# A fused sliding-window attention and gMLP kernel: layout of the transposed x, clearing of the V ring, key evictions on two engines, and the place of the root steps

## The chip, the cores and the metric

The kernel runs on one core of one Trainium2 chip. The metric is the device time of one execution in microseconds, the median of three runs. The core has five engines with instruction streams of their own that wait for one another by semaphores: TensorE (PE in the profile, its weight loads PEld), VectorE (DVE), ScalarE (ACT), GpSimd (POOL) and SyncE (SP, which issues most DMA transfers here).

## The reference

```python
def _A_ref(x, wqkv, wo):                      # H = 32 heads of 16, W = 256
    qkv = (x @ wqkv).reshape(B, S, 3, H, Dh)  # S = 2048, D = 512
    scores = einsum('bhqd,bhkd->bhqk', q, k) * Dh ** -0.5
    scores = where(0 <= i - j < W, scores, -1e9)
    return einsum('bhqk,bhkd->bhqd', softmax(scores), v) @ wo
def _B_ref(x, w_in, w_sp, b_sp, w_out):       # F = 1376, Fh = 688
    z = gelu(x @ w_in)                        # tanh form
    z1, z2 = z[..., :Fh], layernorm(z[..., Fh:])
    g = einsum('ts,bsf->btf', w_sp, z2) + b_sp[None, :, None]
    return (z1 * g) @ w_out
xn = layernorm(x)
return x + _A_ref(xn, wqkv, wo) + _B_ref(xn, w_in, w_sp, b_sp, w_out)
```

All inputs are bfloat16.

## The kernel before

The 2048 tokens are 16 blocks of 128 (NB). The order of the instructions on each engine is written out by hand (`manual_schedule`): every engine executes its instructions in the order in which the Python code emits them, and the framework adds the semaphore waits that the tiles' reads and writes need. There are two parts.

**Prologue** (L230 to L438 of the source, inside one `with` that holds the PSUM pools ps_z and ps_t). x is loaded in pairs of blocks (L249 to L255) and w_in in four parts (c = 0 to 3, L258), two of them from ACT's queue and the rest from SP's. SP's queue then takes wqkv (L261), two transposed loads of w_sp (wspT, L221), wo (L264) and w_out (L265, L268). 14 matmuls on a zero tile `warm` run on PE meanwhile (L273).

For each block DVE takes mean and variance (`stat_steps`, L302 and L303), makes 1/sqrt and normalises x in place (L307). The first four blocks take the root from ACT (L347); blocks 4 to 15 take it four at a time from `rsqrt_steps` (L107), a chain of twelve small DVE instructions: three to set up (L111, L112, L116) and three Newton rounds (L123, L124, L128). `weave(a, b)` (L135) emits two lists alternately; the loop at L375 weaves the roots of one group with some statistics of the next. PE transposes the normalised block in four 128x128 pieces into a PSUM tile `tp` (L316) and ACT copies it to `xnT` (L319).

PE multiplies each block with w_in in two halves (`do_z`, `z_part`, L328: eight matmuls for one half of one block, called a z tile here), and ACT writes gelu of it to z1_all or z2_all (L344). The loop at L408 goes through the z tiles: both halves of blocks 1 to 8, then the second halves (z2) of 9 to 15, then their first halves. In it are dealt out:
- the transposes of later blocks;
- nine early units of the attention for the first 512 tokens: k0, q0, k1, q1, k2, q2, k3, q3 and v0 (`unit_k`, `unit_q`, `unit_v`; the number is the group of eight heads G). Each is four matmuls into a PSUM tile `me` from the same pool as `tp` (two banks, tag "t"), and evictions. A key unit is written twice to `k_ring`, for even and odd heads (e = 0, 1), each multiplied with a 0/1 column `emask`; in before both on DVE (L168). A query unit is copied by ACT (L183); v0 by DVE in four pieces (L202);
- the `side` list, one entry after each z tile from block 5: `clear_strips` (L95) zeroes strips of five E buffers, and `clear_v` (L224) zeroes one of five slots of the V ring and sets its columns of ones (L225, L227), all on DVE;
- the statistics of z2 (`z2_stats`, L207 and L208). After the eighth block the twelve root steps for blocks 0 to 7 follow in one piece (L429 in the print below), after the sixteenth those for 8 to 15, woven with the normalisation `z2_norm` (L211) of blocks 0 to 7.

The early evictions in before, as they stand:

```python
for e in range(2):
    dst = k_ring[:, G, o : o + 8, e, :]
    if on_act:
        nc.scalar.activation(out=dst, in_=m, func=ACT.Copy, scale=emask[:, e : e + 1])
    else:
        nc.vector.tensor_scalar(
            out=dst, in0=m, scalar1=emask[:, e : e + 1], scalar2=None, op0=ALU.mult
        )
...
u(a, 0, on_act=(u is unit_q), early=True)
```

**Main loop** (L650). 128 steps of two key half blocks each: four scores matmuls into S (`quad`, L534), exp by ACT into an E buffer (L544), a mask by DVE (L560), attention times V (`unit_av`, L575, L591, L592). A planner with fixed costs (C_P and so on, L604) fills PE between them with the remaining q, k and v units, the w_sp products (`unit_g`, L458, evicted at L464) and the output products (L492, L500, L504).

Of the kernel before, what the change touches and what calls it, by code (L numbers as in the profile page):

```python
# [8 lines left out]
P = 128  # L9
BF = mybir.dt.bfloat16  # L10
F32 = mybir.dt.float32
# [4 lines left out]
S_TOK = 2048  # L16
# [28 lines left out]
def kernel(  # L45
# [18 lines left out]
    ident = pers.tile([P, P], BF, name="ident")  # L64
    xnT = pers.tile([P, NDC, S_TOK], BF, name="xnT")
    wqkv = pers.tile([P, NDC, 3 * D], BF, name="wqkv")
# [7 lines left out]
    mask2 = pers.tile([P, 2, HK], BF, name="mask2")  # L74
    eps_t = pers.tile([P, 1], F32, name="eps_t")
    emask = pers.tile([P, 2], F32, name="emask")
    esel = pers.tile([P, 4], F32, name="esel")
# [75 lines left out]
    def unit_k(G, grp, on_act=False, early=False):  # L153
        m = m_tile(early=early)
        for c in range(NDC):
            nc.tensor.matmul(  # L156
                m, lhsT=wqkv[:, c, D + G * P : D + (G + 1) * P],
                rhs=xnT[:, c, grp * 512 : (grp + 1) * 512],
                start=(c == 0), stop=(c == NDC - 1),
            )  # L160
        o = (grp % 2) * 8
        m = m.rearrange("p (a k) -> p a k", k=HK)
        for e in range(2):
            dst = k_ring[:, G, o : o + 8, e, :]
            if on_act:
                nc.scalar.activation(out=dst, in_=m, func=ACT.Copy, scale=emask[:, e : e + 1])
            else:
                nc.vector.tensor_scalar(  # L168
                    out=dst, in0=m, scalar1=emask[:, e : e + 1], scalar2=None, op0=ALU.mult
                )  # L170

    def unit_q(G, grp, on_act=False, early=False):
        m = m_tile(early=early)
        for c in range(NDC):
            nc.tensor.matmul(  # L175
                m, lhsT=wqkv[:, c, G * P : (G + 1) * P],
                rhs=xnT[:, c, grp * 512 : (grp + 1) * 512],
                start=(c == 0), stop=(c == NDC - 1),
            )
        o = (grp % 2) * 512  # L180
        dst = q_ring[:, G, o : o + 512]
        if on_act:
            nc.scalar.copy(out=dst, in_=m)  # L183
        else:
            nc.vector.tensor_copy(out=dst, in_=m)

    def unit_v(n, on_act=False, early=False):
        m = m_tile(early=early)
        for c in range(NDC):
            nc.tensor.matmul(  # L190
                m, lhsT=xnT[:, c, n * P : (n + 1) * P], rhs=wqkv[:, c, 2 * D : 3 * D],
                start=(c == 0), stop=(c == NDC - 1),
            )
# [9 lines left out]

    def z2_stats(n):
        st = sml.tile([P, 2, nc.vector.BN_STATS_DIM], F32, name="st2")
        for j in range(2):
            nc.vector.bn_stats(out=st[:, j, :], in_=z2_all[:, n, j * 344 : (j + 1) * 344])  # L207
        nc.vector.bn_aggr(out=mv2[:, n, :], in_=st[:].rearrange("p a b -> p (a b)"))  # L208

# [13 lines left out]

    def clear_v(k):  # L224
        nc.vector.memset(v_ring[:, k], 0.0)  # L225
        for e in range(2):
            nc.vector.memset(v_ring[e * HK : (e + 1) * HK, k, :, :, e, DH : DH + 1], 1.0)  # L227


    with tc.tile_pool(name="win_pool", bufs=1) as winp, tc.tile_pool(  # L230
# [4 lines left out]
        w_in_sb = winp.tile([P, NDC, F], BF, name="w_in_sb")  # L235
        warm = winp.tile([P, 512], BF, name="warm")
        nc.vector.memset(warm[:], 0.0)
# [6 lines left out]
        for n2 in range(NB // 2):  # L244
# [11 lines left out]
            if n2 == 1:  # L256
                for c in range(NDC):
                    (nc.scalar if c < 2 else nc.sync).dma_start(  # L258
                        out=w_in_sb[:, c, :], in_=B_w_in[c * P : (c + 1) * P, :]
                    )  # L260
        nc.sync.dma_start(out=wqkv[:], in_=A_wqkv.rearrange("(c p) f -> p c f", p=P))  # L261
        load_wsp(0)
        load_wsp(1)
# [8 lines left out]
        for i in range(14):  # L272
            nc.tensor.matmul(wm[:], lhsT=warm[:, 0:P], rhs=warm[:], start=True, stop=True)  # L273

# [37 lines left out]
        def transpose_x(n):  # L312
            tp = ps_t.tile([P, NDC, P], BF, name="tp", tag="t")
            xn = xs_tiles.pop(n)
            for c in range(NDC):
                nc.tensor.transpose(  # L316
                    out=tp[:, c, :], in_=xn[:, c * P : (c + 1) * P], identity=ident[:]
                )
            nc.scalar.copy(out=xnT[:, :, n * P : (n + 1) * P], in_=tp[:])  # L319

# [4 lines left out]
        def z_part(zp, n, half, c):  # L325
            f0 = half * FH
            for lo, hi in Z_RANGES:
                nc.tensor.matmul(  # L328
                    zp[:, lo:hi],
                    lhsT=xnT[:, c, n * P : (n + 1) * P],  # L330
                    rhs=w_in_sb[:, c, f0 + lo : f0 + hi],
# [38 lines left out]
        norm_root(3)  # L370
        tiny = sml.tile([P, 1], F32, name="tiny")
        nc.scalar.activation(out=tiny[:], in_=eps_t[:], func=ACT.Gelu_apprx_tanh)

        weave(stat_steps(4, 8), [])
        for lo, hi, nxt in ((4, 8, 10), (8, 12, 14), (12, NB, NB)):  # L375
            weave(stat_steps(lo + 2 if lo > 4 else hi, hi), [])
            weave(rsqrt_steps(rstdx[:, lo:hi], mvx[:, lo:hi, 1], hi - lo), stat_steps(hi, nxt))
            for n in range(lo, hi):
                norm_apply(n)
            if lo == 4:  # L380
# [6 lines left out]
                )  # L387
                nc.vector.tensor_copy(out=b_all[:], in_=b_bf[:])

        early = [(unit_k, 0), (unit_q, 0), (unit_k, 1), (unit_q, 1), (unit_k, 2), (unit_q, 2),  # L390
                 (unit_k, 3), (unit_q, 3), (unit_v, 0)]
        side = [lambda eb=eb: clear_strips(eb) for eb in e_bufs]
        side += [lambda k=k: clear_v(k) for k in range(VRING)]
        stats_done = 0

        first = [(0, 0), (0, 1), (1, 0)]
        zt = [z_tile() for _ in first]
        for c in range(NDC):
            for zp, (n, half) in zip(zt, first):
                z_part(zp, n, half, c)  # L400
        transpose_x(2)
        for zp, (n, half) in zip(zt, first):
            gelu(n, half, zp)
        order = [(1, 1)] + [(n, h) for n in range(2, Z_BOTH) for h in range(2)]
# [3 lines left out]
        for i, (n, half) in enumerate(order):  # L408
# [5 lines left out]
            if n >= 6 and (half == 1 or i >= len(order) - 2) and early:  # L414
# [3 lines left out]
                else:  # L418
                    u(a, 0, on_act=(u is unit_q), early=True)
            if n >= 5:  # L420
                if side:
                    side.pop(0)()
                ready = n if half == 1 else (n if n < Z_BOTH else NB)
                for _ in range(1 if half == 0 and n < Z_BOTH else 2):
                    if stats_done < ready:
                        z2_stats(stats_done)
                        stats_done += 1
                        if stats_done == 8:
                            weave(rsqrt_steps(rstd2[:, 0:8], mv2[:, 0:8, 1], 8), [])  # L429
                        if stats_done == NB:  # L430
                            weave(
                                rsqrt_steps(rstd2[:, 8:NB], mv2[:, 8:NB, 1], NB - 8),
                                [lambda n=n: z2_norm(n) for n in range(8)],
                            )
                            for k in range(8, NB):
                                z2_norm(k)
        assert not early and not side and stats_done == NB and next_t == NB

# [163 lines left out]


    C_P, C_G, C_OU, C_OO, C_AV = 870, 145, 1300, 870, 620  # L604
    GAPS = NB * 8
# [145 lines left out]
```

## Time and profile before

| what | us |
|---|---|
| median of three runs (308.41 to 309.09) | 308.58 |
| the profiled execution | 307.7 |
| its span, first to last instruction | 306.0 |
| PE busy | 286.2 (94%) |
| DVE busy | 203.2 (66%) |
| ACT busy | 196.0 (64%) |
| first scores matmul of the main loop (L534) starts at | 72.31 |
| first matmul of v0 starts at | 61.11 |
| wqkv is issued at, and lands after | 7.79, 11.8 |

The page gives the busy share of each engine in 40 slices of 7.65 us. PE's row begins with 8 7 7 9 9 7 3 8 9 7 and has a 9 in every slice after that but the last. The row of the granted TensorE clock has a 6 in the seventh slice and an 8 in the last, and a 9 in all others. In the chain that ended last PE has 77% of the span, DVE 12% and DMA 5%; DVE and most of the DMA stand in the first quarter of it.

An instruction's time in the timelines runs from its start to its modelled end; matmuls overlap, so that the distance from one start to the next is shorter than the duration. "A <-B" in brackets is the engine's idle time before the instruction and what ended it.

### The profile page before, as it was taken

How to read it: one execution, taken by the hardware profiler on the slowest of the kernel's cores; microseconds unless marked ns; L12 is line 12 of the kernel's file. 1: busy time of each engine (PE TensorE's matmuls, PEld its weight loads, DVE VectorE, ACT ScalarE, POOL GpSimd, SP SyncE). 2: the span in 40 equal slices, each digit the busy share in tenths (PEclk: the TensorE clock that was granted, in tenths of full speed). 3: DMA queues.
4: the chain of work that ended last, by engine and by line, in shares of the span. 5: the costliest groups of instructions: out<-in, count | busy, mean ns of one | idle time of the engine just before them, and what ended most of it. 6: DMA issues, size and time to landing. Idle time of an engine off the chain costs nothing.

```text
span 306.0 us, 7754 instructions
## 1 busy us (share of the span) xinstructions
PE 286.2 (94%) x3214; PEld 164.1 (54%) x3214; DVE 203.2 (66%) x505; ACT 196.0 (64%) x316; POOL 12.0 (4%) x31
## 2 busy tenths in 40 slices
PE   8779973897999999999999999999999999999994
PEld 3446531453454555555655555565555656556761
DVE  6698988999876676645658666876563647453441
ACT  2767632457777777777767767767767767676400
POOL 5000000000000000000000000000000000000000
PEclk9999996999999999999999999999999999999998
DMA  7996000000041416251526124150735144712513
GB/s 264 291 247 198 2 1 0 1 2 0 0 89 42 95 38 145 12 134 43 62 51 141 43 45 86 38 104 13 99 80 117 54 96 82 173 42 62 113 23 91
DMA packets 62482, 24.63 MB, mean 81 GB/s; under 512 B 55616, under 2 KB 60912, under 8 KB 62448
## 3 DMA queue, kind: packets, MB, share of 16 engines
q1 hardware_dynamic: 61200, 21.21, 31.7%
q0 software_dynamic: 816, 2.10, 2.8%
q10 hardware_dynamic: 432, 0.84, 0.7%
q8 instruction: 25, 0.41, 0.6%
q14 instruction: 9, 0.07, 0.1%
HBM read 8.41 MB, written 2.10 MB: 34 GB/s over the span
## 4 chain that ended last, share of the span: by engine, by line
PE 77%; DVE 12%; DMA 5%; ACT 2%; issue 1%; SPq 1%
PE gf L458 25%; PE o_t L575 11%; PE S L534 11%; PE m L492 6%; PE zp L328 5%; PE m L190 4%; PE m L500 4%; PE m L156 4%; PE m L175 4%; DMA xs<-in_A_x_dram 3%; DVE st L302 2%; DVE st L207 2%; DMA wspT<-in_B_w_sp_dram 2%; DVE xs L307 1%; DMA oT<-o_norm 1%
## 5 line engine op out<-in xcount | busy, mean ns | idle before, releaser
L544 ACT ACTIVATE E<-S 128x640 bf16<-128x640 f32 (+4 forms) x256 | 157.6, 668 | 60.4 <-PE S L534 60.2
L458 PE MATMUL gf<-z_all,wspT 128*128 128x344 bf16 x512 | 90.3, 310 | 0.2 <-DMA wspT<-in_B_w_sp_dram 0.2
L458 PEld LDWEIGHTS <-wspT 128*128 128x128 bf16 x512 | 44.8, 98 | 30.6 <-DMA wspT<-in_B_w_sp_dram 0.6
L575 PEld LDWEIGHTS <-E 128*128 128x128 bf16 x1440 | 45.4, 96 | 10.5 <-DVE E L560 0.6
L560 DVE TENSOR_TENSOR E<-E,mask 128x1024 bf16<-128x1024 bf16 (+1 forms) x64 | 41.7, 651 | 7.7 <-ACT E L544 7.5
L575 PE MATMUL o_t<-v_ring,E 128*128 128x34 bf16 x1440 | 46.0, 177 | 0.0
L534 PE MATMUL S<-q_ring,k_ring 32*128 32x320 bf16 (+4 forms) x576 | 43.9, 280 | 2.0 <-ACT E L544 1.1
L328 PE MATMUL zp<-w_in_sb,xnT 128*128 128x512 bf16 (+1 forms) x256 | 41.5, 314 | 1.8 <-ACT z_all L344 1.3
L464 DVE SCALAR_TENSOR_TENSOR u_sb<-gf,b_all,z_all 128x344 bf16<-128x344 f32 x32 | 18.4, 574 | 24.7 <-PE gf L458 24.6
L328 PEld LDWEIGHTS <-xnT 128*128 128x128 bf16 x256 | 22.6, 100 | 18.0 <-issue 2.8
L534 PEld LDWEIGHTS <-k_ring 32*128 32x128 bf16 x576 | 16.5, 91 | 25.8 <-issue 23.2
L202 DVE CAST v_ring<-m 64x256 bf16<-64x256 f32 x60 | 25.4, 423 | 6.9 <-PE m L190 6.3
L344 ACT ACTIVATE z_all<-zp 128x688 bf16<-128x688 f32 x32 | 23.2, 748 | 4.8 <-PE zp L328 4.8
L319 ACT COPY xnT<-tp 128x512 bf16<-128x512 bf16 x16 | 9.4, 586 | 24.3 <-PE tp L316 24.3
L504 DVE TENSOR_TENSOR out_sb<-m,x_ch 128x512 bf16<-128x512 f32 x13 | 9.0, 692 | 20.8 <-PE m L500 20.8
L168 DVE TENSOR_SCALAR k_ring<-m,emask 128x512 bf16<-128x512 f32 x24 | 16.9, 746 | 6.7 <-PE m L156 6.6
L480 POOL DMA_DIRECT2D x_ch<-in_A_x_dram x16 | 8.6, 540 | 285.8 <-DVE rsum L591 147.3
L492 PE MATMUL m<-w_out_sb,uT 128*128 128x512 bf16 x78 | 19.1, 381 | 0.0
L591 DVE RECIPROCAL rsum<-o_t 128x16 f32<-128x16 f32 x32 | 8.1, 254 | 11.8 <-PE o_t L575 11.7
L190 PE MATMUL m<-wqkv,xnT 128*128 128x512 bf16 x60 | 15.6, 382 | 0.0
L207 DVE BATCH_NORM_STATS2 st<-z_all 128x6 f32<-128x344 bf16 x32 | 14.5, 494 | 0.1
L592 DVE TENSOR_TENSOR o_norm<-o_t,rsum 128x256 bf16<-128x256 f32 x32 | 13.6, 425 | 1.1
(66 smaller groups left out, 183.3 us busy)
## 6 DMA issues: line engine op xcount, KB each, us to landing
x_ch<-in_A_x_dram POOLq DMA_DIRECT2D x16, 128.0 KB, 2.5
out_dram<-out_sb SPq DMA_DIRECT2D x16, 128.0 KB, 1.7
xs<-in_A_x_dram SPq DMA_DIRECT2D x7, 256.0 KB, 8.9
wqkv<-in_A_wqkv_dram SPq DMA_DIRECT2D x1, 1536.0 KB, 11.8
w_in_sb<-in_B_w_in_dram ACTq DMA_DIRECT2D x2, 344.0 KB, 5.1
w_in_sb<-in_B_w_in_dram SPq DMA_DIRECT2D x2, 344.0 KB, 5.8
w_out_sb<-in_B_w_out_dram SPq DMA_DIRECT2D x1, 640.0 KB, 5.8
wo_sb<-in_A_wo_dram SPq DMA_DIRECT2D x1, 512.0 KB, 4.0
```

The costliest lines, as they stand in the source:

```text
L190: nc.tensor.matmul(m, lhsT=xnT[:, c, n * P : (n + 1) * P], rhs=wqkv[:, c, 2 * D : 3 * D], start=(c == 0), stop=(c == NDC - 1),)
L202: nc.vector.tensor_copy(out=dst, in_=sr)
L207: nc.vector.bn_stats(out=st[:, j, :], in_=z2_all[:, n, j * 344 : (j + 1) * 344])
L328: nc.tensor.matmul(zp[:, lo:hi], lhsT=xnT[:, c, n * P : (n + 1) * P], rhs=w_in_sb[:, c, f0 + lo : f0 + hi], start=(c == 0), stop=(c == NDC ...
L344: nc.scalar.activation(out=dst[:, n, :], in_=zp[:, 0:FH], func=ACT.Gelu_apprx_tanh)
L458: nc.tensor.matmul(gf[:, 0:GH], lhsT=wsp_tiles[n][:, c, :], rhs=z2_all[:, c, cols], start=(c == 0), stop=(c == NB - 1),)
L464: nc.vector.scalar_tensor_tensor(out=u_sb[:, cols], in0=gf[:, 0:GH], scalar=b_all[:, n : n + 1], in1=z1_all[:, n, cols], op0=ALU.add, op1= ...
L492: nc.tensor.matmul(fo, lhsT=uT[:, c, :], rhs=w_out_sb[:, c, :], start=(c == 0), stop=False)
L534: nc.tensor.matmul(S[:, i, d0 : d0 + w], lhsT=k_ring[32 * s : 32 * s + 32, G, a % (2 * QRING), :, :].rearrange("p e k -> p (e k)"), rhs=q_ ...
L544: nc.scalar.activation(out=data(E, j, j + 2)[:, :, 0:ncol], in_=tiles[pr][:, :, 0:ncol], func=ACT.Exp, scale=SM_SCALE,)
L560: nc.vector.tensor_tensor(out=reg, in0=reg, in1=mk, op=ALU.min)
L575: nc.tensor.matmul(o_t[:, 4 * g2 + s, :, :].rearrange("p e d -> p (e d)"), lhsT=E_tiles[(a // 2, G)][:, base : base + P], rhs=v_ring[:, (a ...
```

## The change

- `xnT` is laid out block by block: [128, 16 blocks, 4, 128] instead of [128, 4, 2048]. ACT's copy writes 512 columns in one run; `unit_k` and `unit_q` read the four blocks of a group in four runs of 128 columns instead of one of 512.
- The five slots of the V ring are zeroed by five transfers on SP's queue from the zero tile `warm` (widened from 512 to 544 columns), after wqkv and ahead of the w_sp loads. The columns of ones are set by two DVE memsets over all slots. These and the five `clear_strips` stand before the loop over the z tiles; the `side` list is gone.
- w_in's part 3 is issued after x blocks 4 and 5 instead of before them.
- Early key units are evicted with e = 0 on DVE and e = 1 on ACT.
- The statistics of x blocks 8 and 9 follow the first group's roots instead of being woven into them.
- The gelus of z tiles (0,0) and (0,1) are emitted before the transposes of block 2 and their copy.
- The root steps for z2 of blocks 0 to 7 are dealt out, three woven with the statistics of each following block; the last root steps and norms follow the loop.
- `tiny`, the one-column tile with which the gelu table is loaded early, is used once more with Exp between the prologue and the main loop.

```diff
-    xnT = pers.tile([P, NDC, S_TOK], BF, name="xnT")
+    xnT = pers.tile([P, NB, NDC, P], BF, name="xnT")
...
-                rhs=xnT[:, c, grp * 512 : (grp + 1) * 512],
+                rhs=xnT[:, 4 * grp : 4 * grp + 4, c, :],
...
-            if on_act:
+            if on_act and e == 1:
                 nc.scalar.activation(out=dst, in_=m, func=ACT.Copy, scale=emask[:, e : e + 1])
...
-    def z2_stats(n):
+    def z2_steps(n):
         st = sml.tile([P, 2, nc.vector.BN_STATS_DIM], F32, name="st2")
-        for j in range(2):
-            nc.vector.bn_stats(out=st[:, j, :], in_=z2_all[:, n, j * 344 : (j + 1) * 344])
-        nc.vector.bn_aggr(out=mv2[:, n, :], in_=st[:].rearrange("p a b -> p (a b)"))
+        steps = [
+            lambda j=j: nc.vector.bn_stats(
+                out=st[:, j, :], in_=z2_all[:, n, j * 344 : (j + 1) * 344]
+            )
+            for j in range(2)
+        ]
+        steps.append(
+            lambda: nc.vector.bn_aggr(
+                out=mv2[:, n, :], in_=st[:].rearrange("p a b -> p (a b)")
+            )
+        )
+        return steps
...
-    def clear_v(k):
-        nc.vector.memset(v_ring[:, k], 0.0)
-        for e in range(2):
-            nc.vector.memset(v_ring[e * HK : (e + 1) * HK, k, :, :, e, DH : DH + 1], 1.0)
...
-                for c in range(NDC):
+                for c in range(3):
                     (nc.scalar if c < 2 else nc.sync).dma_start(
                         out=w_in_sb[:, c, :], in_=B_w_in[c * P : (c + 1) * P, :]
                     )
+            if n2 == 2:
+                nc.sync.dma_start(out=w_in_sb[:, 3, :], in_=B_w_in[3 * P : 4 * P, :])
         nc.sync.dma_start(out=wqkv[:], in_=A_wqkv.rearrange("(c p) f -> p c f", p=P))
+        for k in range(VRING):
+            nc.sync.dma_start(
+                out=v_ring[:, k].rearrange("p a g e d -> p (a g e d)").rearrange(
+                    "p (r c) -> p r c", c=544
+                ),
+                in_=warm[:].unsqueeze(1).to_broadcast([P, 2, 544]),
+            )
         load_wsp(0)
...
-            nc.scalar.copy(out=xnT[:, :, n * P : (n + 1) * P], in_=tp[:])
+            nc.scalar.copy(out=xnT[:, n], in_=tp[:])
...
-        for lo, hi, nxt in ((4, 8, 10), (8, 12, 14), (12, NB, NB)):
-            weave(stat_steps(lo + 2 if lo > 4 else hi, hi), [])
+        for lo, hi, nxt in ((4, 8, 8), (8, 12, 14), (12, NB, NB)):
+            weave(stat_steps(14 if lo == 12 else lo, hi) if lo > 4 else [], [])
             weave(rsqrt_steps(rstdx[:, lo:hi], mvx[:, lo:hi, 1], hi - lo), stat_steps(hi, nxt))
...
+        for eb in e_bufs:
+            clear_strips(eb)
+        for e in range(2):
+            nc.vector.memset(v_ring[e * HK : (e + 1) * HK, :, :, :, e, DH : DH + 1], 1.0)
...
-        side = [lambda eb=eb: clear_strips(eb) for eb in e_bufs]
-        side += [lambda k=k: clear_v(k) for k in range(VRING)]
         stats_done = 0
+        chain = []
...
+        for zp, (n, half) in zip(zt[:2], first[:2]):
+            gelu(n, half, zp)
         transpose_x(2)
-        for zp, (n, half) in zip(zt, first):
-            gelu(n, half, zp)
+        gelu(1, 0, zt[2])
...
-                    u(a, 0, on_act=(u is unit_q), early=True)
+                    u(a, 0, on_act=True, early=True)
             if n >= 5:
-                if side:
-                    side.pop(0)()
...
-                    if stats_done < ready:
-                        z2_stats(stats_done)
-                        stats_done += 1
-                        if stats_done == 8:
-                            weave(rsqrt_steps(rstd2[:, 0:8], mv2[:, 0:8, 1], 8), [])
...
+                    if stats_done == ready:
+                        break
+                    weave(z2_steps(stats_done), [chain.pop(0) for _ in range(3) if chain])
+                    stats_done += 1
+                    if stats_done == 8:
+                        chain += rsqrt_steps(rstd2[:, 0:8], mv2[:, 0:8, 1], 8)
...
+    nc.scalar.activation(out=tiny[:], in_=eps_t[:], func=ACT.Exp)
```

More of the change, by code (lines that the diff above doesn't have):

```diff
@@ L75 @@
     eps_t = pers.tile([P, 1], F32, name="eps_t")
+    tiny = pers.tile([P, 1], F32, name="tiny")
     emask = pers.tile([P, 2], F32, name="emask")
@@ L176, in unit_q @@
                 m, lhsT=wqkv[:, c, G * P : (G + 1) * P],
-                rhs=xnT[:, c, grp * 512 : (grp + 1) * 512],
+                rhs=xnT[:, 4 * grp : 4 * grp + 4, c, :],
                 start=(c == 0), stop=(c == NDC - 1),
@@ L190, in unit_v @@
             nc.tensor.matmul(
-                m, lhsT=xnT[:, c, n * P : (n + 1) * P], rhs=wqkv[:, c, 2 * D : 3 * D],
+                m, lhsT=xnT[:, n, c, :], rhs=wqkv[:, c, 2 * D : 3 * D],
                 start=(c == 0), stop=(c == NDC - 1),
@@ L235 @@
         w_in_sb = winp.tile([P, NDC, F], BF, name="w_in_sb")
-        warm = winp.tile([P, 512], BF, name="warm")
+        warm = winp.tile([P, 544], BF, name="warm")
         nc.vector.memset(warm[:], 0.0)
@@ L272 @@
         for i in range(14):
-            nc.tensor.matmul(wm[:], lhsT=warm[:, 0:P], rhs=warm[:], start=True, stop=True)
+            nc.tensor.matmul(wm[:], lhsT=warm[:, 0:P], rhs=warm[:, 0:512], start=True, stop=True)
         for e in range(2):
@@ L329, in z_part @@
                     zp[:, lo:hi],
-                    lhsT=xnT[:, c, n * P : (n + 1) * P],
+                    lhsT=xnT[:, n, c, :],
                     rhs=w_in_sb[:, c, f0 + lo : f0 + hi],
@@ L370 @@
         norm_root(3)
-        tiny = sml.tile([P, 1], F32, name="tiny")
         nc.scalar.activation(out=tiny[:], in_=eps_t[:], func=ACT.Gelu_apprx_tanh)
         weave(stat_steps(4, 8), [])
-        for lo, hi, nxt in ((4, 8, 10), (8, 12, 14), (12, NB, NB)):
-            weave(stat_steps(lo + 2 if lo > 4 else hi, hi), [])
+        for lo, hi, nxt in ((4, 8, 8), (8, 12, 14), (12, NB, NB)):
+            weave(stat_steps(14 if lo == 12 else lo, hi) if lo > 4 else [], [])
             weave(rsqrt_steps(rstdx[:, lo:hi], mvx[:, lo:hi, 1], hi - lo), stat_steps(hi, nxt))
@@ L418 @@
                 else:
-                    u(a, 0, on_act=(u is unit_q), early=True)
+                    u(a, 0, on_act=True, early=True)
             if n >= 5:
-                if side:
-                    side.pop(0)()
-                ready = n if half == 1 else (n if n < Z_BOTH else NB)
+                ready = n if half == 1 or n < Z_BOTH else NB
                 for _ in range(1 if half == 0 and n < Z_BOTH else 2):
-                    if stats_done < ready:
-                        z2_stats(stats_done)
-                        stats_done += 1
-                        if stats_done == 8:
-                            weave(rsqrt_steps(rstd2[:, 0:8], mv2[:, 0:8, 1], 8), [])
[L430 to L437, printed above, removed]
+                    if stats_done == ready:
[4 more added lines that the diff above has]
+                        chain += rsqrt_steps(rstd2[:, 0:8], mv2[:, 0:8, 1], 8)
+        weave(
+            rsqrt_steps(rstd2[:, 8:NB], mv2[:, 8:NB, 1], NB - 8),
+            [lambda n=n: z2_norm(n) for n in range(8)],
+        )
+        for k in range(8, NB):
+            z2_norm(k)
+        assert not early and not chain and stats_done == NB and next_t == NB
     ps_s = ctx.enter_context(tc.tile_pool(name="ps_s", bufs=2, space=bass.MemoryType.PSUM))
```

## The prediction, made before the changed kernel was run

> **What bounds the kernel now.** I read the page first (its busy share of PE in 40 slices and the granted clock), then the chain of waits over the first 76 us, then the timelines of PE, DVE and ACT there, and last the built program's order and waits of both kernels.
>
> The page shows PE busy nine tenths or more in every slice from the eleventh (76 us) to the last but one, so only the prologue has much to give, and the change edits only that. Its deepest hole, the seventh slice (busy 3 tenths, clock 6 tenths), is this, by stretches of time (columns: stretch, its length, then PE, PEld, DVE, ACT and POOL busy, granted clock, DMA share, GB/s):
>
> ```profile
> 31.00:45.00 14.00, 12.65 (x88) 7.30 (x87) 12.64 (x41) 7.46 (x12) 0.00 (x0) 1.00 0.01 2
> 45.00:50.00 5.00, 0.26 (x4) 0.14 (x2) 4.38 (x18) 0.00 (x0) 0.00 (x0) 0.80 0.00 0
> 50.00:55.00 5.00, 4.33 (x18) 2.03 (x17) 4.03 (x11) 1.82 (x3) 0.00 (x0) 0.52 0.00 0
> 55.00:62.00 7.00, 5.65 (x39) 3.04 (x37) 6.39 (x16) 3.74 (x6) 0.00 (x0) 1.00 0.00 1
> ```
>
> PE stands still for nearly 5 us while DVE works, and then runs 5 us at about half the clock. The chain of waits names what it stands for (start, us, what):
>
> ```profile
> 44.88 0.95 DVE st L207 x2
> ...
> 46.09 0.18 DVE rs_v L111
> ...
> 48.48 1.33 DVE k_ring L168 x2
> 49.81 0.04 issue
> 49.86 0.60 PE tp L316 x4
> ...
> 51.12 1.87 PE me L175 x4
> 52.98 2.12 PE zp L328 x8
> ```
>
> DVE serves V clears, statistics and twelve root steps before it empties the PSUM tile of the second early key unit (k1). The next transposes need that bank. From PE's timeline, three instructions that the sum below starts from:
>
> ```profile
> 33.33 1.03 PE L175 MATMUL me<-xnT,wqkv 128*128 128x512 bf16 x4
> 39.84 1.02 PE L175 MATMUL me<-xnT,wqkv 128*128 128x512 bf16 x4 [0.67 <-ACT xnT L319]
> 49.86 0.59 PE L316 MATMUL tp<-ident,xs 128*128 128x128 bf16 x4 [4.75 <-DVE k_ring L168]
> ```
>
> The first is unit q0. It does not wait in before, though k0's tile is emptied only 3 us later, by the third line of this excerpt of DVE's and ACT's timelines:
>
> ```profile
> 31.28 0.27 DVE L96 MEMSET E<- 128x256 uint32 x1
> 34.39 0.59 ACT L183 CAST q_ring<-me 128x512 bf16<-128x512 f32 x1
> 36.36 1.36 DVE L168 TENSOR_SCALAR k_ring<-me,emask 128x512 bf16<-128x512 f32 x2
> 72.70 1.28 ACT L544 ACT_TABLE_LOAD   x1 [0.45 <-PE S L534]
> 74.00 2.49 ACT L544 ACTIVATE E<-S 128x640 bf16<-128x640 f32 x4
> ```
>
> **The change, part by part.** What PE executes and in which order is the same in both built programs, so PE gains or loses only by waits.
>
> *Root steps and V clears.* DVE loses five V clears (0.96 us, with their two small memsets and gaps about 1.6 us each, 41.68 to 44.88 for two) and the block of twelve root steps (46.09 to 48.48, 2.4 us). In after the steps lie between statistics, three to each. The wait of 4.75 us at 49.86 goes, with its slow clock: regular, tp at 41.86 is followed by the next at 44.95; here the distance from 44.88 to 54.94 is 10.0 instead of 3.1, so the stall costs 6.9 us (4.9 of standing, 2.0 of half clock).
>
> *Key evictions on two engines: where the stall goes.* The built program's waits show a new link. ACT's half (e=1) of k_ring waits for DVE's half (e=0) of the same unit, and the matmuls of q0 wait for ACT's half, because the early tiles now alternate strictly between two banks. In before q0 waits only for ACT's copy of the last transposes. So what is late next is q0, and DVE's arrival at k0 decides. Behind the waiting ACT instruction stand the copy of xnT block 9 and two gelus, which PE needs after q0; they take 0.59 + 2 x 0.75 us and are done while q0 and z(8,0) run.
>
> DVE reaches k0 at 36.36 in before, without a gap since 11.17, when x blocks 4 and 5 land. In after, ahead of it:
> - statistics of blocks 8 and 9 are no longer woven into the first roots of x. Roots alone take 27.51 to 29.89 (2.38), two pairs of statistics 19.53 to 21.17 (1.64), woven they took 14.50 to 17.81 (3.31): +0.71;
> - two more E strips (31.28 to 31.59, 0.31 each): +0.62;
> - two memsets of ones, 64x160. The trace has 64x32 (0.085, 0.24 to the next) and 128x1088 of the same type (0.965), so one is between 0.1 and 0.3 us with its gap on top: +0.2 to +0.9, I take 0.5, near the small row.
>
> k0 on DVE: 36.36 + 0.71 + 0.62 + 0.5 = 38.2. DVE's half takes 0.74 (median of L168), then ACT's half. An ACT eviction of that shape with a scale is not in the trace; the copy L183 takes 0.59, gelu on 688 columns 0.75, so 0.59 to 0.75, and I take the equal shape. With 0.05 and 0.04 for the hand-overs q0 starts at 39.6, against 33.33: 6.3 us late. PE has reached that point by 32.4, since x block 4 is normalised 0.9 earlier, and stands for 7 us.
>
> From q0 to v0 the work at full clock is 7 units of 0.86 (33.33 to 34.19), 8 z tiles of 1.17 and 6 transposes of 0.23: 16.8 us. Before, it took 33.33 to 61.12 = 27.8: the 16.8, five waits of 0.84 for the copy (39.00 to 39.84), 4.9 and 2.0. After, the copy is no longer waited for, but q1, q2 and q3 wait for ACT's half: 0.65 + 0.38 + 0.74 + 0.59 + 0.09 = 2.45 us after the unit's start, while PE comes back after 0.86 + 1.17 + 0.23 = 2.26: 0.2 each, 0.6. The stall is long enough for half clock again. In before the clock was half from 47.97 to 54.79, 4.9 us past the stall's end; the same here costs about 2.3 (bounds: none of it, and 3.4 if a whole 6.8 us of busy time fell in it). So v0 starts at 39.6 + 16.8 + 0.6 + 2.3 = 59.3, against 61.12: **-1.8 us**.
>
> *Exp table.* The load starts at 72.70, after the first scores. In after a one-column Exp pulls it to the end of the last gelu (72.25 in before's time), so the first exponentials start at 72.25 + 1.28 + 0.2 = 73.75 instead of 74.00. PE waits there for ACT (0.58 and 0.28 us), so **-0.25** (bounds 0 and -0.45).
>
> *Transfers in the queue of SP.* V clears are five transfers, 1.39 MB, issued after wqkv and ahead of both wspT, wo and w_out. wqkv lands at 19.6 (issued 7.79, 11.8 to landing), the queue moved 248 GB/s between 11 and 31 us, so V lands near 25.3 and the rest up to 6 us later than before (wspT 24.4 to 30, w_out 28 to 34). First uses are at 73.4 (gf) and 94.3 (m): hidden. DVE asks for V at 33.6, 8 us of cover. w_in's last part passes behind x blocks 4 and 5, about 1 us later; what follows on PE has 7 us of slack before q0. If that slack were gone it would cost that 1 us.
>
> *Nothing at all:* x by blocks (ACT's copy 0.59 writes 512 columns as does q's copy, 0.59; PE reads 4 runs of 128 where it read 512: no row shows such a read, bounds below); first gelus ahead of a copy, and x blocks 4, 5 landing earlier: hidden by the same 7 us, since DVE's statistic of block 6 (12.79 in before) follows the landing of blocks 6 and 7 (12.7) either way.
>
> Sum: -1.8 - 0.25 = -2.0. Span 306.0 to 304.0. The profiled execution took 307.7, 0.9 below the median 308.58; the difference is applied to the median: **306.6 us**.
>
> [...]
>
> **Rivals.**
> 1. *The link does not bind*: ACT's half does not wait, or q0 finds its bank free. For it: before's q0 passed k0 by. Against: the built waits. Then PE goes from 32.4 with 16.8 + 0.6 to v0 at 49.8, 11.3 earlier; DVE, at 38.2, still has four key halves, twelve statistics of 1.05, root steps and v0 (about 19 us), then norms of 7.4, to end at 64.6 against 75.2. So about -10: 298.5.
> 2. *Slower: the ones wait for V's transfers.* DVE's memset of ones stands ahead of every z2 statistic and k0. It decides from a landing after 33.6; the gain is used up at 35.6, and each us more is a us lost. For it: transposed SBUF copies of 128 KB took 2.7 us each, five of 278 KB in series at that rate take 29 us, landing at 49: +13, 322. At twice that rate it lands at 34 and costs 0.4. Against: 248 GB/s.
> 3. *Slower: strided reads of x.* 128 matmuls of k and q; 16 ns more on each 216 uses up the gain, 10% more costs 2.8: 309.4. For it only that no row shows the form.
> 4. *No difference that shows*: the half clock reaches its upper bound (+1.1) and ACT's half takes 0.75 each of four times (+0.64): 308.3.
>
> **How the numbers follow.** Likeliest case, 306.6: 0.65, its own range 305.4 to 308.2 from the bounds (ones -0.3/+0.4, ACT half +0.64, clock -0.6/+1.1, Exp -0.2/+0.25). Rival 1: 0.10; rival 2: 0.07; rival 3: 0.05; rival 4: 0.13. The range 305.0 to 309.3 leaves out rival 1 and most of 2. About 0.2% (0.6 us) is what a measurement can tell from no change. Faster: 0.58 of the likeliest, 0.10 of rival 1: 0.68. Same: 0.06 and 0.07 of rival 4: 0.13. Slower: the rest, 0.19.
>
> **What would show it.** Right: one PE wait of about 7 us at the q0 matmuls near 32 to 40 us, released by ACT's k_ring, itself released by DVE; the 4.75 us wait gone; q units waiting 0.2 us; half clock in the sixth slice; first Exp near 72; v_ring landed by 26. Wrong: no wait at q0 (rival 1), DVE idle before the memset of ones (rival 2), me matmuls above 379 ns at full clock (rival 3).

## The result, and the profile after

The changed kernel takes 306.32 us (median of six runs, 305.93 to 307.18), the kernel before 308.92 in six runs beside it (308.41 to 310.21): a ratio of 0.9914, 95% interval 0.9891 to 0.9937. Its profiled execution took 305.99 us, with a span of 304.3 against 306.0.

The page of the changed kernel: busy share of PE and granted clock in 40 slices, now of 7.61 us.

```profile
PE   8879269998999999999999999999999999999994
...
PEclk9999959999999999999999999999999999999999
```

The hole has moved from the seventh slice to the fifth, and is a little deeper (2 tenths); the half clock stands in the sixth. The busy times by stretches, columns as before:

```profile
31.00:40.00 9.00, 1.66 (x14) 1.02 (x13) 7.76 (x30) 0.00 (x0) 0.00 (x0) 0.86 0.18 62
40.00:45.00 5.00, 4.22 (x18) 2.01 (x18) 4.08 (x13) 3.09 (x6) 0.00 (x0) 0.57 0.00 0
45.00:50.00 5.00, 4.77 (x32) 2.70 (x32) 1.94 (x7) 4.09 (x7) 0.00 (x0) 1.00 0.01 3
```

From 31 to 40 us PE has 1.66 us of work and ACT none at all, while DVE is busy. ACT stood beside PE in the hole of before too (0.00 us busy from 45 to 50), but this hole is longer. The chain of waits of the changed kernel says what for (start, us, what):

```profile
33.30 0.27 DVE E L97
33.61 0.49 issue
34.10 0.19 DVE v_ring L405
34.29 0.59 issue
34.88 0.19 DVE v_ring L405
35.09 0.95 DVE st L208 x2
...
39.39 0.63 DVE k_ring L169
40.04 0.70 ACT k_ring L167
40.74 0.04 issue
40.78 1.86 PE me L176 x4
```

DVE clears strips, sets the ones, takes four statistics of z2, and only then empties its half of k0. ACT's half follows it, and q0's matmuls follow ACT's half. PE's timeline has the wait itself, and the small one of every later query unit:

```profile
40.78 1.86 PE L176 MATMUL me<-xnT,wqkv 128*128 128x512 bf16 x4 [8.12 <-ACT k_ring L167]
48.50 1.02 PE L176 MATMUL me<-xnT,wqkv 128*128 128x512 bf16 x4 [0.17 <-ACT k_ring L167]
```

ACT's timeline has the idle time behind DVE, and the table of Exp, now loaded before the first scores are there:

```profile
40.04 0.69 ACT L167 ACTIVATE k_ring<-me,emask 128x512 bf16<-128x512 f32 x1 [10.02 <-DVE k_ring L169]
...
71.36 1.28 ACT L619 ACT_TABLE_LOAD   x1
72.65 0.20 ACT L619 ACTIVATE tiny<-eps_t 128x1 f32<-128x1 f32 x1
72.76 2.47 ACT L559 ACTIVATE E<-S 128x640 bf16<-128x640 f32 x4
```

The first exponentials start at 72.76 instead of 74.00. The main loop carries these 1.24 us unchanged to 258 us; there a wait for a w_sp load, 0.6 us in before, is gone, and the lead becomes 1.52; the tail makes it 1.7.

So the large saving on DVE (194.7 us busy instead of 203.2) came to little, because a stall of 4.75 us was exchanged for one of 8.12 in another place: q0 starts 7.45 us later than in before. A gain is left because the way from q0 to v0 became 8.4 us shorter (27.8 to 19.4); the stall at k1 has gone from it, and so have five waits for the copy of xnT, 0.84 us each.

### The profile page after: what moved, and what is told of

It reads as the page before. It is cut to its first block, busy times and chain, and to the rows that moved or that the text cites. A ratio compares the mean times of both kernels' runs of the same rounds, so it can differ in the third digit from the quotient of the medians.

```text
span 304.3 us, 7723 instructions
## 1 busy us (share of the span) xinstructions
PE 283.2 (93%) x3186; PEld 163.8 (54%) x3214; DVE 194.7 (64%) x488; ACT 198.2 (65%) x321; POOL 12.0 (4%) x31
## 4 chain that ended last, share of the span: by engine, by line
PE 80%; DVE 9%; DMA 5%; ACT 2%; issue 2%; SPq 0%; DVEq 0%
PE gf L473 26%; PE o_t L590 12%; PE S L549 11%; PE m L507 6%; PE zp L342 5%; PE m L191 4%; PE m L515 4%; DMA xs<-in_A_x_dram 4%; PE m L176 4%; PE m L157 4%; DVE st L316 2%; PE me L176 2%; DVE xs L321 1%; DMA oT<-o_norm 1%; DVE st L208 1%
## 5 line engine op out<-in xcount | busy, mean ns | idle before, releaser
L479 DVE SCALAR_TENSOR_TENSOR u_sb<-gf,b_all,z_all 128x344 bf16<-128x344 f32 x32 | 18.4, 574 | 24.9 <-PE gf L473 24.8
L507 PE MATMUL m<-w_out_sb,uT 128*128 128x512 bf16 x67 | 17.3, 380 | 1.2 <-issue 1.0
L333 ACT COPY xnT<-tp 128x512 bf16<-128x512 bf16 x16 | 9.4, 587 | 10.2 <-PE tp L330 10.2
L191 PE MATMUL m<-wqkv,xnT 128*128 128x512 bf16 x51 | 14.6, 381 | 0.8 <-issue 0.5
## 6 DMA issues: line engine op xcount, KB each, us to landing
v_ring<-warm SPq DMA_DIRECT2D x5, 272.0 KB, 10.6
```

Of the source, the lines that this page charges most:

```text
L191: nc.tensor.matmul(m, lhsT=xnT[:, n, c, :], rhs=wqkv[:, c, 2 * D : 3 * D], start=(c == 0), stop=(c == NDC - 1),)
L479: nc.vector.scalar_tensor_tensor(out=u_sb[:, cols], in0=gf[:, 0:GH], scalar=b_all[:, n : n + 1], in1=z1_all[:, n, cols], op0=ALU.add, op1= ...
L507: nc.tensor.matmul(fo, lhsT=uT[:, c, :], rhs=w_out_sb[:, c, :], start=(c == 0), stop=False)
```

## The experiments

Each kernel was timed against the kernel before on the same chip, whose medians lay between 308.3 and 308.9. Theory: PE loses its time because an eviction stands behind other work on DVE, and the split makes the loss larger by tying ACT and the next query unit to DVE's half. Rivals: the split brings part of the gain; or the gain lies in the other parts of the change. One thing varies between all profiled executions: DVE's last normalisation of x starts between 29.6 and 30.7 us (31.4 in e2), by when x has landed (17.8 us behind the end of DVE's last wait for x in the changed kernel, e1, e3, e7, e8, e9 and e12), and moves what follows by as much.

### Who empties the key units

**e1: no split, keys on DVE.**

```diff
-                    u(a, 0, on_act=True, early=True)
+                    u(a, 0, on_act=(u is unit_q), early=True)
```

> The changed kernel with both halves of the early keys on DVE again. Theory (the link from DVE's half to ACT's half to q0 decides): q0 no longer waits and starts near 32.4 instead of 40.8; the stall moves to the transposes of block 11, which need k0's bank. DVE still reaches k0 at 39.3, both halves end at 39.3 + 0.66 + 0.74 = 40.7, PE is there at about 38, so it stands for about 3 us instead of 8.1. DVE gets 4 x 0.7 us more work, of which the part in its idle time before k1 to k3 is free. First exponentials at 71 to 72 instead of 72.8, span 302.5 to 304.0 against 304.3. Rival (the division of the keys is what brings the gain): the stall comes back to at least the 4.75 us of before with nothing won at q0, span 305.5 or more.

Measured: 302.74 us, ratio 0.9815 (0.9784 to 0.9846), span 301.2. From PE's timeline of e1:

```profile
31.89 1.03 PE L176 MATMUL me<-xnT,wqkv 128*128 128x512 bf16 x4
...
40.13 0.38 PE L330 MATMUL tp<-ident,xs 128*128 128x128 bf16 x4 [2.62 <-DVE k_ring L169]
```

q0 passes k0 by and runs nine microseconds earlier. DVE is about as late as in the changed kernel (both halves of k0 are written by 40.1), but now PE meets it only at later transposes, for 2.62 us. Without the split the span is 3.1 us shorter, though DVE has 0.7 us more to do at every key unit. That is more than was forecast: first Exp came at 68.28 (said 71 to 72), the span lies 1.3 us below its range. At first Exp the lead over the changed kernel is 4.5 us; 1.1 us of it are given back near 257 us, where PE stands for a w_sp load.

**e12: the halves exchanged, ACT first.**

```diff
-            if on_act and e == 1:
+            if on_act and e == 0:
```

> The changed kernel with the halves exchanged: ScalarE writes its half first, VectorE the other after it, so that VectorE is the last to release the bank of a key unit. Theory (which engine releases a bank last decides which bank the next unit takes; in the built program q0 then takes the bank that the transposes left, as in e1, and ScalarE's queue no longer stands behind VectorE): q0 starts near 32 without a wait, PE stands later, at transposes near 40, for 2 to 3 us until VectorE has emptied k0, one window of half clock, first Exp 67 to 69, span 299 to 301. Rival (any split ties the two queues together): q0 waits 6 us or more again, span 303 or more.

Measured: 300.50 us, ratio 0.9743 (0.9717 to 0.9768), span 298.8, first Exp at 66.14. From PE's timeline of e12:

```profile
32.15 1.03 PE L176 MATMUL me<-xnT,wqkv 128*128 128x512 bf16 x4
...
39.73 0.38 PE L330 MATMUL tp<-ident,xs 128*128 128x128 bf16 x4 [1.97 <-DVE k_ring L169]
```

The same split with its order turned round, and q0 does not wait: while DVE is late, it isn't the sharing that hurts but which half comes last. Where ACT comes last (the changed kernel, e2, e5), q0 waits for k0's bank; here, in e1 and in before, where DVE comes last and late, q0 takes the bank that the transposes left, and k0's is asked for by later transposes. The last engine alone does not decide it: in e11 below DVE comes last and in time, and q0 waits for k0's bank there. What does decide it is not settled. The stall of 1.97 us brought no half clock (q1's four matmuls behind it took 1.02 us, against 1.87 in e1), where the theory had expected a stretch of it; first Exp and span lie 0.9 and 0.2 us below what it gave.

**e9: both halves on ACT, DVE's queue as it was.**

```diff
-            if on_act and e == 1:
+            if on_act:
```

> The changed kernel with both halves of every early key eviction on ScalarE, and VectorE's queue as long as it is there. Theory (the time lost in the first 60 us is PE waiting for an eviction that stands behind other work on VectorE): q0 starts before 34 with a wait of at most 1.5 us, no window of half clock, the key evictions hold the q units back by 0.2 to 0.9 us each, v0 starts between 49 and 52 (60.20 in the changed kernel, 51.32 in e5), the first Exp 12.56 later as in both, span 231.6 after that: 293 to 296. Rival (ScalarE becomes the bound: gelus and copies of x stand behind the second half): new waits of PE for ScalarE add up to 5 us or more, span 298 or more.

Measured: 295.72 us, ratio 0.9584 (0.9559 to 0.9610), span 294.1: the fastest kernel of the study. From PE's and ACT's timelines of e9:

```profile
32.06 1.03 PE L176 MATMUL me<-xnT,wqkv 128*128 128x512 bf16 x4
42.75 1.02 PE L176 MATMUL me<-xnT,wqkv 128*128 128x512 bf16 x4 [0.22 <-ACT k_ring L167]
```

```profile
29.70 1.27 ACT L167 ACTIVATE k_ring<-me,emask 128x512 bf16<-128x512 f32 x2
```

ACT begins to empty k0 as soon as its matmuls end (28.64 + 1.03 = 29.67). Between 20 and 60 us no wait of PE above 0.25 us is left, and v0 starts at 49.66 instead of 60.20. ACT does 2.3 us more over the whole kernel (200.5 us) and did not become the bound. The work on DVE and its order were left as they are but for the key halves; only the tie to it was cut.

**e2: the kernel before with the split alone.**

```diff
-            if on_act:
+            if on_act and e == 1:
...
-                    u(a, 0, on_act=(u is unit_q), early=True)
+                    u(a, 0, on_act=True, early=True)
```

> The kernel before with one edit: early keys e = 0 on DVE, e = 1 on ACT. Theory: DVE reaches k0 at 36.4 as before, q0 waits until 36.4 + 0.7 + 0.7 + 0.1 = 37.9 (from 33.3, 4.5 us), and the block of root steps with the V clears still holds k1 until about 48; q1 then waits about 1 to 2 us more. The 4.75 us wait at 49.9 goes. Stall for stall about the same as before: span 305 to 307.5 against 306.0, no clear difference. Rival (the division brings the gain): span 304.5 or less.

Measured: 310.75 us, ratio 1.0078 (1.0051 to 1.0105), span 310.1: a miss. Two lines, from DVE's and from PE's timeline of e2:

```profile
12.70 0.69 DVE L302 BATCH_NORM_STATS2 st<-xs 128x6 f32<-128x512 bf16 x1 [3.64 <-DMA xs<-in_A_x_dram]
```

```profile
50.78 1.86 PE L175 MATMUL me<-xnT,wqkv 128*128 128x512 bf16 x4 [5.60 <-ACT k_ring L166]
```

The forecast had 4.5 us of waiting at q0 and 1 to 2 us at q1. Measured were 1.59 at q0 and 5.60 at q1: V clears and the block of root steps still stand ahead of k1's first half, and now q1 waits for it through ACT, 5.60 us instead of 4.75 at the transposes. The profiled execution also had x blocks 4 and 5 land 1.5 us later than in before (12.70 against 11.17), with a half clock early on (mean granted clock 0.83 from 11 to 31 us, 1.00 in before), so its span of 310.1 is not the price of the split alone; the median, 2.1 us above before, says that the split alone brings nothing and costs something. How much of the 2.1 is the landing of x stays open.

### What stands ahead of k0 on DVE

**e3: strips cleared twice**, meant as 1.57 us more ahead of k0.

```diff
         for eb in e_bufs:
             clear_strips(eb)
+            clear_strips(eb)
```

> The changed kernel with the five E strips cleared twice, 1.57 us more on DVE ahead of k0. Theory: every microsecond by which DVE is later at k0 is paid in full: q0 at 42.3 instead of 40.8, span 304.3 + 1.6 = 305.9, up to 307 where the half clock lasts a window longer. Rival (DVE's place before k0 is covered, the stall has another cause): span 304.3 within 0.4.

Measured: 307.99 us, ratio 0.9987 (0.9966 to 1.0008), span 305.6. From PE's timeline of e3:

```profile
41.78 1.87 PE L176 MATMUL me<-xnT,wqkv 128*128 128x512 bf16 x4 [10.08 <-ACT k_ring L167]
```

The wait grows by 1.96 us. Both clearings together took 3.53 us (31.08 to 34.61) where one took 1.57 in the changed kernel, so that DVE had 1.96 more ahead of k0 and the wait grew by just that. q0 started only 1.0 later, at 41.78, since x was normalised 0.96 earlier in this execution. The span grows by 1.3: with this much more on DVE the change is no gain that can be measured.

**e4: strips at the very start, ones on POOL**, 3 us less ahead of k0.

```diff
         nc.vector.memset(w_out_sb[:, NFC - 1, :], 0.0)
+        for eb in e_bufs:
+            clear_strips(eb)
...
-        for eb in e_bufs:
-            clear_strips(eb)
         for e in range(2):
-            nc.vector.memset(v_ring[e * HK : (e + 1) * HK, :, :, :, e, DH : DH + 1], 1.0)
+            nc.gpsimd.memset(v_ring[e * HK : (e + 1) * HK, :, :, :, e, DH : DH + 1], 1.0)
```

> The changed kernel with the E strips cleared at the very start on DVE, in its idle time from 1.6 to 3.5, and the columns of ones set by POOL. Takes 1.57 + 1.48 = 3.05 us off DVE ahead of k0. Theory: DVE at k0 at 36.3, q0 at 37.7 instead of 40.8, span 304.3 - 3.1 = 301.2 (301 to 302). Rival (covered): 304.3 within 0.4.

Measured: 302.92 us, ratio 0.983 (0.980 to 0.986), span 300.5. From PE's and POOL's timelines of e4:

```profile
36.82 1.86 PE L176 MATMUL me<-xnT,wqkv 128*128 128x512 bf16 x4 [5.53 <-ACT k_ring L167]
```

```profile
23.21 1.80 POOL L405 MEMSET v_ring<- 64x160 bf16 x2 [18.89 <-DMA v_ring<-warm]
```

The wait shrinks by 2.6 us, where 3.05 were taken away (1.57 and 1.48), and its end, q0's start, comes 3.96 earlier. The span falls by 3.8. Some of it is luck: x blocks 6 and 7 reached DVE at 11.48 here and at 12.86 in the changed kernel's profiled execution. POOL's line dates the V transfers: landed by 23.2. The move has a price, too: while POOL writes the ones, four normalisations of x on DVE (from 23.87) take 1.94 us instead of 1.38.

**e6: the price of the ones.** The ones go to POOL, and DVE writes two memsets of the same size to a tile that no transfer writes.

```diff
-            nc.vector.memset(v_ring[e * HK : (e + 1) * HK, :, :, :, e, DH : DH + 1], 1.0)
+            nc.gpsimd.memset(v_ring[e * HK : (e + 1) * HK, :, :, :, e, DH : DH + 1], 1.0)
+            nc.vector.memset(dum[e * HK : (e + 1) * HK, :, 0:1], 1.0)
```

> The ones of the V ring are written by GpSimd, and at their old place VectorE writes two strided memsets of the same 160 elements to a tile that no transfer writes. Theory (the idle 0.49 and 0.59 us ahead of VectorE's two memsets are the price of waiting for the V transfers, which landed long before): the two memsets take 0.3 to 0.5 us in all instead of 1.48, VectorE empties k0 near 38.3 instead of 39.31, q0 starts near 39.7, span near 303.3 and the time 1 us below the changed kernel's 306.3. Rival (the idle time belongs to a memset of this form, wherever it writes): the two still take 1.3 us or more, and the span stays at 304.3.

Measured: 305.82 us, ratio 0.9907 (0.9875 to 0.9938), span 303.6. From DVE's timeline of e6:

```profile
32.89 0.47 DVE L407 MEMSET dum<- 64x160 bf16 x2
33.38 0.94 DVE L209 BATCH_NORM_STATS2 st<-z_all 128x6 f32<-128x344 bf16 x2
```

From the last strip to the first statistic it is now 0.49 us, where the chain of the changed kernel has 1.48 (33.61 to 35.09). So 1.0 of the 1.48 goes when the two memsets write another tile. That this is a wait for the transfers, as the theory has it, is not shown. The profile calls the idle time "issue": DVE waited for nothing that it shows, and the last V transfer had landed at 24.9 in the changed kernel, 8.7 us before. And `dum`, a tile of [128, 160, 2], differs in a second way: the elements written lie 4 bytes apart, those of the V ring 68; in before, where no transfer writes the V ring, DVE idles 0.15 to 0.17 us ahead of its memsets of ones, which have 32 elements instead of 160. k0 came 1.7 earlier on DVE (37.60; 0.7 of it because x was normalised earlier in this execution, and this in spite of 1.0 us that four normalisations lost beside POOL's memsets), the first Exp 1.17, the span 0.7: half clock lasted longer here (4.6 us behind the stall against 3.5), 20.0 us from q0 to v0 against 19.4.

**e5: z2 statistics later.** e4, and in addition the statistics begin behind k0.

```diff
-            if n >= 5:
+            if n >= 7 or (n == 6 and half == 1):
```

> Beside e4 (strips at the start, ones on GpSimd), VectorE begins the z2 statistics two blocks later, so that its half of the first key eviction (k0) stands ahead of every z2 statistic. Theory (VectorE's lateness at k0 is all that sets the wait of q0): VectorE empties k0 near 32.2 (35.35 in e4), ScalarE's half follows, q0 starts near 33.6 with a wait of 1 to 2 us (5.53 in e4), no window of half clock, first Exp between 63 and 66 (68.62 in e4), span 295 to 298 (300.5 in e4). Rival (the work pushed back is owed later: the evictions of k1 to k3 or the norms of z2 become late instead): q0 is early, but a new wait of 3 us or more stands at a later unit or ahead of the first gating matmuls, and the span is 299 or more.

Measured: 297.74 us, ratio 0.9649 (0.9616 to 0.9682), span 295.6. From DVE's and PE's timelines of e5:

```profile
31.19 0.74 DVE L169 TENSOR_SCALAR k_ring<-me,emask 128x512 bf16<-128x512 f32 x1
```

```profile
32.70 1.02 PE L176 MATMUL me<-xnT,wqkv 128*128 128x512 bf16 x4 [1.53 <-ACT k_ring L167]
```

The split is in place, and its stall is down to 1.53 us without any half clock (q0's matmuls take 1.02 us, against 1.86 in e4). The work that was pushed back cost little: q1 waits 1.08 us for k1 where it waited 0.17 in e4, and first Exp is at 63.88. So the split is dear only while DVE is late.

**e11: e5 without the split.**

```diff
-                    u(a, 0, on_act=True, early=True)
+                    u(a, 0, on_act=(u is unit_q), early=True)
```

> e5 with both halves of the early key evictions on VectorE (no split). Theory (the split brings nothing of its own once VectorE is in time; VectorE idles 0.81 and 1.70 us ahead of k2 and k3 in e5, which covers 0.7 us more each): span within 1 us of e5's 295.6. Rival (a half on ScalarE is worth its 0.7 us at each of four units): span 297 or more.

Measured: 299.06 us, ratio 0.9699 (0.9668 to 0.9730), span 296.5, 0.9 above e5; by medians 1.3. From PE's timeline of e11:

```profile
32.35 1.04 PE L176 MATMUL me<-xnT,wqkv 128*128 128x512 bf16 x4 [1.48 <-DVE k_ring L169]
```

The theory's bound of 1 us holds in the span alone, and narrowly. But v0 (51.55 against 51.32) and first Exp (64.11 against 63.88) come only 0.23 us later than in e5; about 0.5 more is a wait of PE for a w_sp load near 252 us, which e5 does not have. In the prologue, then, the split is worth some 0.2 us with DVE in time.

### The other parts

**e7: without the early Exp.**

```diff
-    nc.scalar.activation(out=tiny[:], in_=eps_t[:], func=ACT.Exp)
```

> The changed kernel without the tiny Exp that loads ScalarE's table ahead of the first scores (it feeds nothing). Theory: the load of 1.28 us waits for the first scores again, the first Exp starts 0.3 us later (73.0 to 73.2 instead of 72.76), the span is 304.6 and the time 306.6. Rival (the load is hidden either way): span 304.3.

Measured: 306.74 us, ratio 0.9945 (0.9917 to 0.9973), span 305.1. From ACT's timeline of e7:

```profile
71.94 1.28 ACT L559 ACT_TABLE_LOAD   x1 [0.45 <-PE S L549]
73.23 2.49 ACT L559 ACTIVATE E<-S 128x640 bf16<-128x640 f32 x4
```

The load waits for the scores again. From v0 (60.35) to the first Exp it is 12.88 us, as in before (61.12 to 74.00); with the early Exp it is 12.56. The Exp is worth 0.32; the medians differ by 0.4, which lies inside their intervals.

**e8: old layout of x, root steps in one block.** The diff undoes the lines of `xnT` shown above, and:

```diff
-                    weave(z2_steps(stats_done), [chain.pop(0) for _ in range(3) if chain])
+                    weave(z2_steps(stats_done), [])
...
-                        chain += rsqrt_steps(rstd2[:, 0:8], mv2[:, 0:8, 1], 8)
+                        weave(rsqrt_steps(rstd2[:, 0:8], mv2[:, 0:8, 1], 8), [])
```

> The changed kernel with the old layout of the transposed x and with the root steps of the first eight z2 statistics in one block instead of dealt out. Theory: the layout is worth nothing (the matmuls of the early units at 379 ns in both layouts), and the block of root steps holds an eviction back by 1 us at most: span 304.3 to 305.3. Rival (either part carries a part of the gain): span above 305.5.

Measured: 306.48 us, ratio 0.9936 (0.9913 to 0.9959), span 304.2. Four matmuls of a key or query unit take 1.02 or 1.03 us in both layouts. q0 came 0.93 us earlier, as x was normalised that much earlier in this execution, and a longer half clock took 0.7 of it back (from q0 to k1 5.84 us against 5.13). Neither part shows while q0 waits for DVE.

**e13: the kernel before with keys on ACT**, everything else of the change left out.

```diff
-                    u(a, 0, on_act=(u is unit_q), early=True)
+                    u(a, 0, on_act=True, early=True)
```

> The kernel before with one edit, the early key evictions on ScalarE, and everything else of the change left out: V clears and root steps stay on VectorE. Theory (the only thing in these parts that PE waits for is the key eviction behind them): the wait of 4.75 us at 49.86 and its half clock go, v0 starts between 50 and 53 (61.12 before), first Exp 63 to 66 (74.00 before), span 295 to 298, below the changed kernel's 304.3. Rival (the clears and the roots hold something else back, such as the norms of z2 ahead of the main loop): first Exp early, but a new wait follows, span 302 or more.

Measured: 304.45 us, ratio 0.9861 (0.9833 to 0.9888), span 301.1 (its profiled execution was the fastest of six). The first half came as expected: v0 at 52.64, first Exp at 65.52. Then the rival took over, from PE's and DVE's timelines of e13:

```profile
71.86 1.02 PE L175 MATMUL m<-xnT,wqkv 128*128 128x512 bf16 x4 [2.88 <-DVE v_ring L202]
```

```profile
67.01 3.04 DVE L211 TENSOR_SCALAR z_all<-z_all,mv,rstd 128x688 bf16<-128x688 bf16 x8
70.07 1.73 DVE L202 CAST v_ring<-m 64x256 bf16<-64x256 f32 x4
```

The V clears and the roots in one piece were not free. They push the norms of z2 back, these end at 70.05 (63.2 in e9), and a V eviction of the main loop stands behind them. The span of 301.1 lies between what the theory (295 to 298) and the rival (302 or more) gave. With the keys on ACT, the other parts of the change are worth 7.0 us of span (301.1 to 294.1), by medians 8.7.

| kernel | span, us | median, us |
|---|---|---|
| before | 306.0 | 308.92 |
| before, keys on ACT (e13) | 301.1 | 304.45 |
| the change, keys on DVE (e1) | 301.2 | 302.74 |
| the change as it is, split | 304.3 | 306.32 |
| the change, keys on ACT (e9) | 294.1 | 295.72 |

## Why the prediction was right, and where its steps were off

It said 306.6 us by one wait that goes and a larger one that comes at q0. Place, releaser and kind of that wait are as said, and e9 shows that the time hangs on it: without it 10 us more are gained. By the terms of the sum:

- **The old stall.** The 4.75 us are gone, and so is the block of root steps ahead of k1; DVE now idles 2.75 us before k1.
- **DVE at k0.** Said 38.2, measured 39.31. Strips began at 32.04, where the term for the statistics put them (31.28 + 0.71 = 31.99). The term that was too small is "two memsets of ones": 0.5, bounds 0.2 to 0.9, measured 1.48. It was sized near a memset of 32 elements with its gap. The two instructions take only 0.19 each; what was too small is the idle time ahead of them, 0.49 and 0.59. On another tile 1.0 of the 1.48 goes (e6); why is open.
- **ACT's half.** 0.59 taken, bound 0.75, measured 0.69. With both, q0 starts at 40.78 instead of 39.6, after a wait of 8.12 instead of 7 us.
- **q0 to v0.** Said 19.7, measured 19.42, by two errors of opposite sign. The three waits cost more than the 0.2 each: the 0.17 in the brackets counts from a modelled end, but q1, q2 and q3 start 0.56 us after their transposes instead of 0.23, so 0.33 each, 1.0 in all instead of 0.6. The half clock took less than the 2.3 that was read from before: it ended at 44.3, so 3.5 us of it fell behind the stall, 1.75 lost. It differs between runs: in e6 and e8, behind the same stall, q0 to k1 took 5.66 and 5.84 us against 5.13 here, so that 4.6 and 4.9 us of half clock were left, and 2.3 and 2.5 were lost.
- **v0.** Said 59.3 (-1.8), measured 60.20 (-0.92): half of the expected gain. q0 is 1.2 late by the ones and ACT's half, and 0.3 of it comes back on the way to v0.
- **Exp.** Said -0.25, measured -0.32 (e7).
- **At nothing.** Layout and dealt-out roots: right for this kernel (e8). V's landing: said near 25.3, measured 24.9 (the last one issued at 14.4, 10.6 to landing); 23.2 and 23.5 where POOL waited for it (e4, e6).

The sum at the first Exp is -1.24 instead of -2.0, and the span -1.7. The difference of 0.46 came after 258 us and was in no term. That the predicted time is nearer than this is luck: the sum promised 0.8 us too much, and the late part of the main loop (0.5) and the place of the two profiled executions (that of before lay 0.9 below the median shown with it, that of after 0.3) made up for it. The 0.3 us between 306.6 and 306.32 are not the accuracy of the sum. Nor does the range of the likeliest case follow from the bounds listed with it: they add up to 305.5 to 309.0, and its -0.6 for the clock is not the lower bound of the term above, where no loss at all is allowed. That -0.6 means a loss of 1.7 us, a term that no run shows ahead of the result; the runs then showed losses of 1.75 (the changed kernel), 2.3 (e6) and 2.5 us (e8).

The rivals: the first (the link does not bind) fell here, but it described what e9 and e12 bring about; it put the time at 298.5, and e12 gave 300.50, e9 295.72. The second (ones that wait for V's transfers) fell as told, no transfer was late; yet its sign, DVE idle before the memsets of ones, did appear, with 0.49 and 0.59 us, though no late transfer was its cause. The third fell with 1.02 us for four matmuls. The fourth gave 308.3, outside what was measured.

## What to carry to other kernels

When an eviction frees a PSUM bank that TensorE will ask for, look at what stands ahead of it in its engine's queue, not at its own duration: 1.3 us of evictions on ACT, whose queue was empty then, beat half of them on each of two (e9 against the change, 10.2 us of span). In these runs a tile that two engines emptied was released by the later one (k0 by ACT in the changed kernel, by DVE in e12), and which of them that is can change which bank the next unit waits for (q0 stood 8.12 us in the changed kernel, not at all in e12), though it does not decide it alone (e11). Work that is taken out of a loop and put ahead of it lands ahead of the loop's first eviction (q0 waited 10.08 us in e3, 5.53 in e4, 1.53 in e5); and two edits can each hide what the other is worth (e13, the keys on ACT alone, brings 4.9 us of span, e1, the other parts alone, 4.8; e9 has both and brings 11.9).

## What the runs showed of the hardware

- **Idle time ahead of a memset.** DVE stood 0.49 to 0.51 and 0.59 to 0.60 us ahead of the two memsets of ones in every run that had them there, though the V transfers had landed long before (8.7 us in the changed kernel). On a tile that no transfer writes, and whose elements lie closer together, the pair took 0.47 us in all (e6). What takes the time is not shown.
- **DVE beside POOL.** In the four runs with the ones on POOL (e4, e5, e6, e11), the four normalisations of x that ran beside its memsets took 1.94, 2.12, 2.38 and 2.12 us on DVE; the group after it took 1.38 in each, and so did the same group in the changed kernel. No run without them shows it; the memsets were not tested for this alone. So what moving the ones took off DVE ahead of k0 cost it 0.6 to 1.0 us earlier on.
- **Half clock in steps.** By the granted clock in the busy times by stretches (twice a stretch's length times what its mean clock is short of 1), the half clock in the prologues lasted close to 3.4 us (e1: mean clock 0.66 from 40 to 45 us; e4: 0.81 from 31 to 40), 6.8 (before: 0.80 from 45 to 50 and 0.52 from 50 to 55; the changed kernel: 0.86 from 31 to 40 and 0.57 from 40 to 45; e2 twice: 0.83 from 11 to 31, then 0.93, 0.50 and 0.92 between 45 and 62) or 10.2 (e3: 0.70 from 31 to 40 and 0.52 from 40 to 45; e6: 0.64 from 31 to 40 and 0.70 from 37.5 to 47.8, of which 2.5 us of half clock are in both). In e13 the two z tiles from 18.54 us took 4.01 us to the next transposes, where the next two took 2.33: 1.68 lost, 3.4 us again. The same stall of 8.1 us had 6.8 in the changed kernel and 10.2 in e6. The busy times by stretches of the changed kernel show the clock at exactly half between two of full clock:

```profile
34.00:37.40 3.40, 0.00 (x0) 0.00 (x0) 2.63 (x9) 0.00 (x0) 0.00 (x0) 1.00 0.00 0
37.50:44.20 6.70, 3.42 (x11) 1.47 (x11) 6.49 (x19) 3.03 (x5) 0.00 (x0) 0.50 0.00 0
44.40:48.00 3.60, 3.55 (x27) 2.14 (x27) 1.03 (x2) 2.15 (x4) 0.00 (x0) 1.00 0.02 5
```

  The first 3.3 us of that half clock cost nothing, since PE stood still; only what lasts past the stall is paid for. A stall of 1.97 us (e12) had no half clock behind it, one of 2.62 (e1) had (1.87 us for q1's matmuls), one of 2.63 earlier in e9 had none (2.33 us for the two z tiles behind it), and one of 2.72 early in e13 had 3.4 us: the length of the stall alone does not decide it.
- **Issuing the V transfers.** The five took SP from 9.27 to 16.06 us: single issues of 0.59 to 1.70 us (median 0.60, as for wqkv with more than five times the bytes of one) and gaps between them. They moved the first w_sp load from 8.84 to 16.11 us, and nothing waited for it.
